# Attention and two gated MLPs on one core: softmax tiles relaid in DRAM, one load a tile, the leftover values loaded once, and a new order of steps

## The chip, the core and the metric

The kernel runs on one core of a Trainium2 chip. The core has a matmul engine (TensorE, "PE" in the profile, its weight loads as "PEld"), three elementwise engines (VectorE "DVE", ScalarE "ACT", GpSimd "POOL") and a queue engine (SyncE "SP") which here issues every transfer between DRAM and the on-chip memory. Sixteen DMA engines carry them out. The metric is device microseconds (us) for one execution. "Slow" and "fast" below mean this time and nothing else.

## What is computed

A batch of 8 sequences of 576 tokens goes through three stages one after the other: attention with 8 heads against keys and values averaged over groups of 8 tokens (so 72 keys a head), an MLP whose hidden layer is gated by a convolution over tokens, and an MLP gated by a learned mix over tokens.

```python
# q, k, v: (8 batches, 8 heads, 576 tokens, 64)
k_p = k.reshape(B, H, 72, 8, D).mean(axis=3); v_p = likewise
attn = softmax(q @ k_p^T / sqrt(D)); attn_out = attn @ v_p
x = attn_out, heads side by side                      # (8, 576, 512)
h = relu(x @ w_in)                                    # 512 -> 1024
x = (h * sigmoid(conv3(h))) @ w_out                   # 1024 -> 512
u, v = halves of gelu(x @ w_in2)                      # 512 -> 512 and 512
v = layernorm(v) * g_ln;  v = w_sg @ v + b_sg         # mix over tokens
out = (u * v) @ w_out2
```

## The kernel before, in words

Work is cut into small steps, each a Python generator that issues a few instructions and yields. A long string, `ORDER`, names which generator goes on next; the first occurrence of a name is its first step, the second its second, and so on. Each engine executes its instructions strictly in that order, the SP queue too, so the string is the schedule of all five queues at once. An instruction that waits holds up all that stand behind it on its own engine.

The names that matter here, for batch b: `s(t,b)` makes the scores of one tile of 128 tokens (the fifth tile, t=4, has 64), the softmax `e` and its normalised copy `en`; its last, ninth, step writes `en` to DRAM. `e(t,b)` brings that tile back with keys on partitions: its first step loads it from DRAM into `xb`, the second turns 32x32 blocks on DVE (L516), the third rounds it on ACT into `eTh` (L520), the fourth makes the rounding error `eTl` on POOL, the fifth does the same for the leftover keys on DVE. Batches 0 and 1 do this with matmuls instead, so all of that holds for batches 2 to 7, 30 tiles. `a(p,b)` multiplies weights and values for a head pair on PE and leaves the MLP's input in `xT`. `q.b` loads a batch's queries in 16 transfers, `p(t,b)` turns them on DVE. `k`, `K` and `v`, `V` load and pool keys and values. With 72 = 64 + 8 keys a head, the last 8 keys of each of the 8 heads form a rest of 64 rows, which `v2.b` loads; it is wanted three times over on different partitions.

`I(f,c)` is the first MLP's input matmul (12 matmuls into `psi`, of which there are two buffers) for 384 tokens with the convolution and gate behind it on ACT and DVE; the DVE instruction of L594 is the last to read the `psi` buffer. `O(f,c)` is its output matmul, nine matmuls. These two fill PE while the attention of a later batch goes on. Letters `y n u d o m` are the second MLP, after all attention.

The DRAM tile `eds[b]` has one row for each token and in it four runs of 192 numbers, one for each quarter of partitions. Its load is four transfers (L510 to L513), one a quarter, each of rows of 192 numbers. The rest of the values is loaded in six transfers (L257 to L260), from four heads each, so that the three copies lie in `raw` at once, 96 partitions by 2; POOL then pools all of it.

Of the kernel before, what the change touches and what calls it, by code (L numbers as in the profile page):

```python
# [8 lines left out]
F32 = mybir.dt.float32  # L9
# [17 lines left out]
def pooled_attention_gated_mlps(  # L27
# [23 lines left out]
    nc = tc.nc  # L51
    w_in, conv_w, w_out, w_in2, w_out2 = (a.bitcast(U32) for a in (w_in, conv_w, w_out, w_in2, w_out2))
    B, H, S, D = q.shape
    POOL = 8
# [4 lines left out]
    NP_ = H // 2  # L59
# [15 lines left out]
    B_DMA = 2  # L75

    const = ctx.enter_context(tc.tile_pool(name="const", bufs=1))
    stat = ctx.enter_context(tc.tile_pool(name="stat", bufs=2))
    work = ctx.enter_context(tc.tile_pool(name="work", bufs=3))
    outp = ctx.enter_context(tc.tile_pool(name="outp", bufs=2))  # L80
    slot = ctx.enter_context(tc.tile_pool(name="slot", bufs=1))
    dram = ctx.enter_context(tc.tile_pool(name="dram", bufs=1, space=bass.MemoryType.DRAM))
    ps1_ctx = ExitStack()
    psum1 = ps1_ctx.enter_context(tc.tile_pool(name="psum1", bufs=1, space=bass.MemoryType.PSUM))

    x2s = [dram.tile([S, DM], F32, name=f"x2s{b}") for b in range(B)]
    eds = [dram.tile([S, 4 * EQ], F32, name=f"eds{b}") for b in range(B)]
    ps2 = {}

    def a_bank():  # L90
        return psum1.tile([128, 512], F32, tag="a", bufs=3, name="psa")

    def i_bank():
        return psum1.tile([128, 512], F32, tag="i", bufs=2, name="psi")

    def o_bank():
        return psum1.tile([128, 512], F32, tag="o", bufs=CT, name="pso")

    def ps_tile():
# [147 lines left out]
    def load_v(b, i, raw):  # L247


        if i < 2:  # L250
            for a in range(4):
                h0, r0 = 4 * i + a % 2, 32 * POOL * (a // 2)
                nc.sync.dma_start(
                    out=raw[32 * a:32 * a + 32, :, :],
                    in_=v[b, h0:h0 + 3:2, r0:r0 + 32 * POOL, :].rearrange("h (j r) d -> j h (r d)", r=POOL))
            return
        for c in range(2):  # L257
            rest = v[b, 4 * c:4 * c + 4, 64 * POOL:S, :].rearrange("h (j r) d -> h j (r d)", r=POOL)
            for x in range(3):
                nc.sync.dma_start(out=raw[32 * x:32 * x + 4 * RJ, c, :], in_=rest)  # L260
# [66 lines left out]
    def t_v(i, b):  # L327
        if b > 1:
            raw = att2.tile([128, 2, 512], F32, tag="raw", name="raw")
        else:  # L330
            raw = staged("q0" if b == 0 and i == 2 else f"st{b}", 2)
        if i == 2 and b < 2:
            nc.sync.dma_start(out=raw[0:64, 0, :],
                              in_=v[b, :, 64 * POOL:S, :].rearrange("h (j r) d -> h j (r d)", r=POOL))
            yield
            ps = a_bank()[0:64, 0:D]
            mm_sum(ps, [(ident[0:64, 0:64], raw[0:64, 0, D * r:D * r + D]) for r in range(POOL)])
            yield
            kv["vr", b] = att1.tile([96, 2, D], F32, tag="vr", name="vr")
            for x in range(3):  # L340
                for c in range(2):
                    nc.scalar.copy(out=kv["vr", b][32 * x:32 * x + 32, c, :], in_=ps[32 * c:32 * c + 32, :])
            return
        load_v(b, i, raw)
        yield
        P = 128 if i < 2 else 96
        ps = None
        if b < 2:
            ps = a_bank()[0:P, 0:2 * D]
            mm_sum(ps, [(ident[0:P, 0:P], raw[0:P, :, D * r:D * r + D]) for r in range(POOL)])  # L350
            yield
        if i < 2 and ("vp", b) not in kv:
            kv["vp", b] = att1.tile([128, NP_, D], F32, tag="vp", name="vp")
        if i == 2:
            kv["vr", b] = att1.tile([96, 2, D], F32, tag="vr", name="vr")
        dst = kv["vr", b] if i == 2 else kv["vp", b][:, 2 * i:2 * i + 2, :]
        if ps is None:
            yield from pool_sum(pool, raw, dst, P)
        else:
            nc.scalar.copy(out=dst, in_=ps.rearrange("p (a d) -> p a d", a=2))  # L360
# [62 lines left out]
    def t_s(t, b):  # L423


        n = TT[t][1]
        qT = qTs.pop((b, t))
        e = sm = m8 = None
        for a in range(2):
            ps = a_bank()  # L430
            for x in range(2):
                p = 2 * a + x
                nc.tensor.matmul(out=ps[0:n, 2 * SP * x:2 * SP * x + 2 * SP], lhsT=qT[:, p, 0:n], rhs=KBT[:, p, :],  # L433
                                 start=True, stop=True)
            yield
            if a == 0:
                e = att2.tile([128, H, SP + 1], F32, tag="e", name="e")
                sm = stat.tile([128, H], F32, tag="sm", name="sm")
                m8 = stat.tile([128, H], F32, tag="mx", name="mx")
                nc.gpsimd.memset(e[:, :, SP:SP + 1], 1e-9)  # L440
                yield
            sv = ps[0:n, 0:4 * SP].rearrange("p (x j) -> p x j", j=SP)
            mx = m8[:, 4 * a:4 * a + 4]
            nc.vector.tensor_reduce(out=mx[0:n], in_=sv, axis=AX.X, op=ALU.max)  # L444
            if b < B_DMA:
                nc.vector.tensor_tensor(out=e[0:n, 4 * a:4 * a + 4, 0:SP], in0=sv, in1=bc(mx[0:n], 2, SP),
                                        op=ALU.subtract)
            else:
                nc.vector.tensor_tensor(
                    out=e[0:n].rearrange("p (x c) j -> p c x j", x=2)[:, 2 * a:2 * a + 2, :, 0:SP],  # L450
                    in0=sv.rearrange("p (c x) j -> p c x j", x=2),
                    in1=bc(mx[0:n].rearrange("p (c x) -> p c x", x=2), 3, SP), op=ALU.subtract)
            yield
        nc.scalar.activation(out=e[0:n, :, 0:SP], in_=e[0:n, :, 0:SP], func=AF.Exp, scale=EXP_SCALE)
        yield
        nc.vector.tensor_reduce(out=sm[0:n], in_=e[0:n], axis=AX.X, op=ALU.add)  # L456
        rs = stat.tile([128, H], F32, tag="rs", name="rs")
        nc.vector.reciprocal(out=rs[0:n], in_=sm[0:n])
        yield
        en = att1.tile([128, H * SP], F32, tag="en", name="en")  # L460
        if b < B_DMA:
            for y in range(2):
                pool.tensor_tensor(
                    out=en[0:n, 0:512].rearrange("p (c y x i) -> p y c x i", c=NP_, y=2, x=2)[:, y],
                    in0=e[0:n].rearrange("p (c x) j -> p c x j", x=2)[:, :, :, 32 * y:32 * y + 32],
                    in1=bc(rs[0:n].rearrange("p (c x) -> p c x", x=2), 3, 32), op=ALU.mult)
            pool.tensor_tensor(out=en[0:n, 512:H * SP].rearrange("p (h j) -> p h j", h=H),
                               in0=e[0:n, :, 64:SP], in1=bc(rs[0:n], 2, RJ), op=ALU.mult)
            es[b, t] = en
            return  # L470
        pool.tensor_tensor(  # L471
            out=en[0:n, 0:512].rearrange("p (y h i) -> p h y i", y=2, h=H),
            in0=e[0:n, :, 0:64].rearrange("p h (y i) -> p h y i", y=2),
            in1=bc(bc(rs[0:n], 2, 2), 3, 32), op=ALU.mult)
        pool.tensor_tensor(
            out=en[0:n, 512:512 + H * RJ].rearrange("p (c x j) -> p x c j", x=2, j=RJ),
            in0=e[0:n, :, 64:SP].rearrange("p (x c) j -> p x c j", x=2),
            in1=bc(rs[0:n].rearrange("p (x c) -> p x c", x=2), 3, RJ), op=ALU.mult)
        yield
        ed = eds[b][TT[t][0]:TT[t][0] + n, :].rearrange("p (a d) -> p a d", a=4)  # L480
        nc.sync.dma_start(out=ed[:, :, 0:128], in_=en[0:n, 0:512].rearrange("p (a d) -> p a d", a=4))
        nc.sync.dma_start(out=ed[:, :, 128:EQ], in_=bc(en[0:n, 512:H * SP], 1, 4))

    def t_e(t, b):
# [26 lines left out]
        for a in range(4):  # L511
            nc.sync.dma_start(
                out=xb[32 * a:32 * a + 32, 0:EQ * G].rearrange("p (g d) -> p g d", d=EQ),  # L513
                in_=eds[b][T, EQ * a:EQ * a + EQ].rearrange("(g i) d -> i g d", i=32))
        yield
        nc.vector.transpose(out=xb[:, 0:EQ * G], in_=xb[:, 0:EQ * G])  # L516
        yield
        m = xb[:, 0:EQ * G].rearrange("p (g c i) -> p c g i", c=NP_ + 2, i=32)
        eh, el = (z[:, :, T].rearrange("p c (g i) -> p c g i", i=32) for z in (eTh, eTl))
        nc.scalar.copy(out=eh, in_=m)  # L520
        yield
# [385 lines left out]
```

## Time and profile before

| | us |
|---|---|
| median of three runs | 1051.41 |
| lowest and highest of them | 1047.47, 1052.53 |
| profiled execution, its own time | 1045.96 |
| its span, first to last instruction | 1044.2 |
| mean granted TensorE clock | 0.974 of full speed |

Busy time in that span: PE 971.6 us (93%), its weight loads 871.4, DVE 673.4 (64%), ACT 440.1 (42%), POOL 363.2 (35%). PE's busy time is an upper picture, since matmuls overlap and their ends are modelled: gaps in it are real, a full slice may still have some slack. The profile's SP rows give the time that issuing a transfer holds the queue; the transfer itself goes on after it. A row's square brackets give the idle time of its engine just before it and what ended that.

### The profile page before, as it was taken

Reading aid. Unit: us, or ns where it says so; the run is one execution under the profiler, and the core shown is the slowest. Engines: PE = TensorE matmul, PEld = TensorE weight load, DVE = VectorE, ACT = ScalarE, POOL = GpSimd, SP = SyncE. Lnnn points to the kernel's source line nnn. Section 1 sums busy time; section 2 is a strip of 40 time slices with the busy share of each in tenths; the row PEclk is TensorE's granted clock in tenths of the full one; section 3 lists DMA queues with packets and bytes.
Section 4 is the critical chain, followed back from the end, with each engine's and each line's share of the span. In section 5 each row is a group of like instructions: output and inputs, shape, how many; then the busy total and the mean of one; then the engine's idle time right before and its main releaser. Section 6 shows DMA issues by size and latency. Waiting matters only on the chain.

```text
span 1044.2 us, 15301 instructions
## 1 busy us (share of the span) xinstructions
PE 971.6 (93%) x5473; PEld 871.4 (83%) x5473; DVE 673.4 (64%) x1190; ACT 440.1 (42%) x872; POOL 363.2 (35%) x485
## 2 busy tenths in 40 slices
PE   5788869999989799899999989999999999999997
PEld 4676758979879699798879869898989898989896
DVE  5868877878778668768559756727272727272523
ACT  3644544756556455556545634313131313130310
POOL 3577587577766466546212201001000100010000
PEclk9899898999999899999999989999999999999999
DMA  9944057366462734514081272232323232312021
GB/s 241 309 132 101 3 129 188 91 151 168 91 169 74 180 87 112 139 39 122 16 234 59 62 199 43 45 92 46 102 45 92 46 102 45 92 23 102 1 81 61
DMA packets 222440, 107.41 MB, mean 103 GB/s; under 512 B 163008, under 2 KB 194780, under 8 KB 222364
## 3 DMA queue, kind: packets, MB, share of 16 engines
q1 hardware_dynamic: 222364, 106.43, 40.4%
q8 instruction: 43, 0.70, 0.3%
q14 instruction: 33, 0.27, 0.1%
HBM read 76.90 MB, written 29.49 MB: 102 GB/s over the span
## 4 chain that ended last, share of the span: by engine, by line
PE 65%; DVE 12%; DMA 7%; POOL 6%; SPq 4%; issue 3%; ACT 3%; DVEq 0%; POOLq 0%; ACTq 0%
PE ps L122 21%; PE psi L116 10%; PE ps L110 6%; PE ps L109 6%; PE ps L111 6%; PE psa L116 3%; PE pso L109 3%; PE pso L111 3%; PE pso L110 3%; DMA xb<-eds 3%; PE psa L433 1%; DVE psi L587 1%; DVE eTh L153 1%; DVE sm L456 1%; DVE psi L588 1%
## 5 line engine op out<-in xcount | busy, mean ns | idle before, releaser
L153 POOL TENSOR_TENSOR hg<-g,hg 128x384 fp32r<-128x384 f32 x96 | 99.4, 1037 | 120.5 <-ACT hg L597 110.2
L767 POOL TENSOR_SCALAR rstd<-mv 128x2 f32<-128x2 f32 (+1 forms) x20 | 8.1, 407 | 367.1 <-DVE mv L764 367.1
L122 PE MATMUL ps<-w2sh,v 128*128 128x288 f32 x512 | 94.3, 296 | 0.0
L587 DVE SCALAR_TENSOR_TENSOR psi<-h,coef,psi 128x384 f32<-128x384 f32 x96 | 58.8, 613 | 47.6 <-ACT psi L585 47.2
L813 DVE SCALAR_TENSOR_TENSOR y<-ps,coef,bsg 128x576 f32<-128x576 f32 x32 | 26.2, 818 | 89.7 <-PE ps L122 89.7
L818 ACT CAST gt<-y 128x576 fp32r<-128x576 f32 (+2 forms) x48 | 23.0, 512 | 128.2 <-DVE y L815 128.2
L122 PEld LDWEIGHTS ps<-w2sh,v 128*128 128x128 f32 x512 | 77.1, 189 | 0.0
L575 ACT ACTIVATE h<-psi 128x386 f32<-128x386 f32 (+1 forms) x96 | 47.2, 491 | 67.3 <-PE psi L116 66.7
L590 ACT ACTIVATE psi<-psi 128x384 f32<-128x384 f32 x96 | 45.5, 474 | 63.1 <-DVE psi L588 62.7
L597 ACT CAST hg<-g 128x384 fp32r<-128x384 f32 x96 | 48.6, 508 | 44.5 <-DVE g L594 37.0
L588 DVE SCALAR_TENSOR_TENSOR psi<-h,coef,psi 128x384 f32<-128x384 f32 x96 | 59.8, 623 | 3.4
L433 PE MATMUL psa<-KBT,qT 128*128 128x144 f32 (+1 forms) x320 | 55.0, 301 | 5.1 <-DVE qT L418 1.6
L594 DVE SCALAR_TENSOR_TENSOR g<-psi,h 128x384 f32<-128x384 f32 x96 | 51.9, 542 | 11.0 <-ACT psi L590 10.6
L585 ACT ACTIVATE psi<-h,coef 128x384 f32<-128x384 f32 x96 | 56.3, 586 | 3.1
L433 PEld LDWEIGHTS psa<-KBT,qT 128*128 128x128 f32 (+1 forms) x320 | 46.0, 185 | 12.7 <-issue 5.1
L122 PE MATMUL ps<-w2sl,v 128*128 128x288 f32 x256 | 54.8, 296 | 0.0
L799 ACT ACTIVATE u<-ps 128x576 f32<-128x576 f32 x32 | 19.9, 652 | 75.6 <-PE ps L122 75.6
L276 POOL TENSOR_TENSOR raw<-raw 128x512 f32<-128x512 f32 (+2 forms) x36 | 44.0, 1224 | 17.7 <-DMA raw<-in_v_dram 8.2
L516 DVE STREAM_TRANSPOSE xb<-xb 128x768 f32<-128x768 f32 (+1 forms) x30 | 26.8, 895 | 35.9 <-DMA xb<-eds 35.6
L444 DVE TENSOR_REDUCE mx<-psa 128x4 f32<-128x288 f32 (+1 forms) x80 | 35.1, 439 | 17.3 <-PE psa L433 17.1
L471 POOL TENSOR_TENSOR en<-e,rs 128x512 f32<-128x512 f32 (+1 forms) x30 | 31.9, 1063 | 41.3 <-DMA eds<-en 22.5
L153 POOL TENSOR_TENSOR eTl<-xb,eTh 128x512 fp32r<-128x512 f32 (+1 forms) x30 | 36.3, 1211 | 23.8 <-ACT eTh L520 18.0
(409 smaller groups left out, 3016.4 us busy)
## 6 DMA issues: line engine op xcount, KB each, us to landing
xb<-eds SPq DMA_DIRECT2D x96, 96.0 KB
xb<-x2s SPq DMA_DIRECT2D x128, 72.0 KB
x2s<-ob SPq DMA_DIRECT2D x32, 256.0 KB
res<-x2s SPq DMA_DIRECT2D x16, 512.0 KB
out_dram<-ob SPq DMA_DIRECT2D x16, 512.0 KB
qb<-in_q_dram SPq DMA_DIRECT2D x96, 72.0 KB
raw<-in_k_dram SPq DMA_DIRECT2D x12, 512.0 KB
raw<-in_v_dram SPq DMA_DIRECT2D x48, 128.0 KB
```

Source lines behind the costliest of these rows:

```text
L109: nc.tensor.matmul(out=out_, lhsT=ah, rhs=bh, start=first, stop=False)
L110: nc.tensor.matmul(out=out_, lhsT=al, rhs=bh, start=False, stop=False)
L111: nc.tensor.matmul(out=out_, lhsT=ah, rhs=bl, start=False, stop=last)
L116: nc.tensor.matmul(out=out_, lhsT=a, rhs=b_, start=(i == 0), stop=(i == n - 1))
L122: nc.tensor.matmul(out=ps[:, hf, 0:HS], lhsT=a, rhs=b_[:, hf * HS:(hf + 1) * HS], start=(i == 0), stop=(i == n - 1),)
L153: eng.tensor_tensor(out=out, in0=in0, in1=hi.bitcast(F32), op=ALU.subtract)
L433: nc.tensor.matmul(out=ps[0:n, 2 * SP * x:2 * SP * x + 2 * SP], lhsT=qT[:, p, 0:n], rhs=KBT[:, p, :], start=True, stop=True)
L585: nc.scalar.activation(out=y, in_=tap(1), func=AF.Copy, scale=cw(1, f))
L587: nc.vector.scalar_tensor_tensor(out=y, in0=tap(0), scalar=cw(0, f), in1=y, op0=ALU.mult, op1=ALU.add)
L588: nc.vector.scalar_tensor_tensor(out=y, in0=tap(2), scalar=cw(2, f), in1=y, op0=ALU.mult, op1=ALU.add)
L594: nc.vector.scalar_tensor_tensor(out=go, in0=y, scalar=1.0, in1=tap(1), op0=ALU.add, op1=ALU.mult)
L597: nc.scalar.copy(out=hg[:, 0, f, :], in_=g)
```

## The change

Three things change in the code. The softmax tiles get one DRAM tile for each batch and token tile, with four blocks, one for each quarter of partitions, and in a block one row of 192 numbers a token. The load is now one transfer: partition i of a quarter takes G consecutive rows of its block (G=4, or 2 for the 64-token tile), so that the 32x32 blocks that DVE turns hold every fourth token. The reading order behind the turn follows: ACT, POOL and DVE read `xb` with the token group innermost, at a distance of 192 numbers (768 bytes), and write `eTh` and `eTl` in token order. The writes to DRAM keep their number and the length of their runs. The rest of the values is loaded once, in one transfer of 64 rows, pooled on 64 partitions into a new tile `vq`, and six ACT copies of 32x64 spread it (batches 0 and 1 did it in that way already, with matmuls for the pooling). And `ORDER` is another string: the same steps but for one more of each `v2.b`, with b from 2 to 7, in another sequence from the 129th step on.

```diff
-ORDER = '''...
- (around e1.5) I6.5 v0.6 s2.5 I5.5 v1.6 v2.6 p4.5 s2.5 I5.5 s3.5 s3.5 I6.5 s2.5 O7.4 I5.5 I6.5 s2.5 e1.5 O7.4 s3.5 I7.5 I6.5 I5.5 k0.7 I6.5 s2.5 I6.5 s3.5 q.6 I6.5 I7.5 e1.5 I0.6 V.5
+ORDER = '''...
+ (around v2.6) I2.5 p3.5 I3.5 s1.5 v1.6 v0.6 I3.5 s2.5 s1.5 I4.5 v2.6 O6.4 O6.4 I3.5 I4.5 s1.5 s2.5 v1.6
...
+ (around e1.5) I4.5 e1.5 I5.5 O7.4 q.6 I6.5 s2.5 I5.5 I5.5 s2.5 s3.5 I5.5 s3.5 I6.5 I5.5 I7.5 s3.5 V.5 I6.5 s3.5 s4.5 s4.5 V.5 e1.5 I7.5
...
-    eds = [dram.tile([S, 4 * EQ], F32, name=f"eds{b}") for b in range(B)]
+    eds = {(b, t): dram.tile([4 * n, EQ], F32, name=f"eds{b}{t}")
+           for b in range(B_DMA, B) for t, (_, n) in enumerate(TT)}
...
     def load_v(b, i, raw):
-        if i < 2:
-            for a in range(4):
...
-            return
-        for c in range(2):
-            rest = v[b, 4 * c:4 * c + 4, 64 * POOL:S, :].rearrange("h (j r) d -> h j (r d)", r=POOL)
-            for x in range(3):
-                nc.sync.dma_start(out=raw[32 * x:32 * x + 4 * RJ, c, :], in_=rest)
...
+        if i == 2:
+            nc.sync.dma_start(out=raw[0:64, 0, :],
+                              in_=v[b, :, 64 * POOL:S, :].rearrange("h (j r) d -> h j (r d)", r=POOL))
+            yield
+            vq = att1.tile([64, D], F32, tag="vq", name="vq")
+            yield from pool_sum(pool, raw[:, 0:1], vq.rearrange("p (a d) -> p a d", a=1), 64)
+            yield
+            kv["vr", b] = att1.tile([96, 2, D], F32, tag="vr", name="vr")
+            for x in range(3):
+                for c in range(2):
+                    nc.scalar.copy(out=kv["vr", b][32 * x:32 * x + 32, c, :], in_=vq[32 * c:32 * c + 32, :])
+            return
...
-        ed = eds[b][TT[t][0]:TT[t][0] + n, :].rearrange("p (a d) -> p a d", a=4)
+        ed = eds[b, t].rearrange("(a p) d -> p a d", a=4)
...
-        for a in range(4):
-            nc.sync.dma_start(
-                out=xb[32 * a:32 * a + 32, 0:EQ * G].rearrange("p (g d) -> p g d", d=EQ),
-                in_=eds[b][T, EQ * a:EQ * a + EQ].rearrange("(g i) d -> i g d", i=32))
+        nc.sync.dma_start(out=xb[:, 0:EQ * G], in_=eds[b, t].rearrange("(p g) d -> p (g d)", g=G))
...
-        m = xb[:, 0:EQ * G].rearrange("p (g c i) -> p c g i", c=NP_ + 2, i=32)
-        eh, el = (z[:, :, T].rearrange("p c (g i) -> p c g i", i=32) for z in (eTh, eTl))
+        m = xb[:, 0:EQ * G].rearrange("p (g c i) -> p c i g", c=NP_ + 2, i=32)
+        eh, el = (z[:, :, T].rearrange("p c (i g) -> p c i g", i=32) for z in (eTh, eTl))
```

Counted over the 30 tiles, `I` and `O` first steps (each some 2 us of PE) that the string puts between a tile's load and its turn: 49 before, 72 after (one for 13 tiles before; two is the least after). Between a tile's write and its load: 77 before, 108 after. Between `q.b` and `p0.b`, batches 2 to 7: 3, 3, 4, 5, 4, 4 before and 4, 5, 6, 6, 4, 6 after. Before, `v2.3`, `v2.4`, `v2.5` and `v2.6` load one `I` or `O` step ahead of the loads of `e0.2`, `e1.3`, `e1.4` and `e1.5`, and no other transfer is issued between the two; after, `v2.3`, `v2.4` and `v2.5` come behind `e1.2`, `e1.3` and `e1.4`, and `v2.6` three steps ahead of `e1.5`. After, the 16 transfers of `q.3`, `q.4`, `q.5` and `q.7` stand four such steps ahead of the loads of `e1.2`, `e1.3`, `e1.4` and `e1.6`.

## Rows read from the trace of the kernel before

**Rows 1.** The page's 40 slices of the span, PE and granted clock, in tenths.
```profile
PE   5788869999989799899999989999999999999997
PEclk9899898999999899999999989999999999999999
```

**Rows 2.** Busy time by stretch: length, then PE, PEld, DVE, ACT, POOL, clock, DMA share, GB/s.
```profile
0.00:128.00 128.00, 98.08 (x588) 82.47 (x588) 97.52 (x176) 62.98 (x148) 75.94 (x113) 0.92 0.62 160
128.00:506.00 378.00, 347.28 (x1825) 310.74 (x1825) 284.94 (x538) 214.20 (x432) 243.14 (x313) 0.97 0.50 121
506.00:624.00 118.00, 111.34 (x543) 97.33 (x543) 81.51 (x139) 59.20 (x121) 21.31 (x21) 0.97 0.43 122
624.00:1044.20 420.20, 414.94 (x2522) 380.91 (x2520) 209.43 (x338) 103.77 (x172) 22.80 (x40) 1.00 0.26 63
```

**Rows 3.** Timeline of PE, 128 to 506 us: start, length, work, [idle before, releaser].
```profile
158.45 0.69 PE L116 MATMUL psi<-xh,wi5hl 128*128 128x388 f32 x1 [6.52 <-DVE g L594]
...
228.93 0.54 PE L116 MATMUL psi<-xh,wi3hl 128*128 128x386 f32 x1 [2.03 <-DVE g L594]
...
285.06 0.44 PE L116 MATMUL psi<-xh,wi5hl 128*128 128x388 f32 x1 [1.85 <-DVE g L594]
...
353.57 0.69 PE L116 MATMUL psi<-xh,wi1hl 128*128 128x386 f32 x1 [7.58 <-DVE g L594]
...
428.64 0.44 PE L116 MATMUL psi<-xh,wi6hl 128*128 128x388 f32 x1 [2.20 <-DVE g L594]
```

**Rows 4.** Who waited for whom, one line (total, times, longest), and DVE's timeline.
```profile
DVE xb L516 <- DMA xb<-eds: 35.6, 19, 6.3
...
152.16 0.98 DVE L516 STREAM_TRANSPOSE xb<-xb 128x768 f32<-128x768 f32 x1 [5.01 <-DMA xb<-eds]
...
348.58 0.98 DVE L516 STREAM_TRANSPOSE xb<-xb 128x768 f32<-128x768 f32 x1 [6.26 <-DMA xb<-eds]
...
423.45 0.71 DVE L418 STREAM_TRANSPOSE qT<-qb 128x512 f32<-128x512 f32 x1 [3.56 <-DMA xb<-eds]
```

**Rows 5.** Timeline of the SP queue: start, time the issues hold it, transfer, count.
```profile
337.82 4.04 SPq L260 DMA_DIRECT2D raw<-in_v_dram  x6
341.99 1.79 SPq L512 DMA_DIRECT2D xb<-eds  x4
...
409.91 11.36 SPq L391 DMA_DIRECT2D qb<-in_q_dram  x16
```

**Rows 6.** Three short stretches behind gaps, columns as in rows 2.
```profile
158.40:164.00 5.60, 5.55 (x17) 5.55 (x18) 3.39 (x7) 2.26 (x5) 2.40 (x4) 0.50 0.63 129
228.90:234.00 5.10, 5.07 (x18) 4.86 (x19) 4.48 (x9) 2.76 (x6) 2.31 (x3) 0.67 0.85 212
353.60:360.00 6.40, 6.40 (x22) 5.56 (x23) 3.31 (x8) 2.06 (x5) 4.37 (x6) 0.59 0.86 159
```

**Rows 7.** The chain that ended last, in order of time: start, length, piece.
```profile
189.32 2.12 PE psi L116 x12
...
343.35 5.11 DMA xb<-eds
...
501.29 1.81 DMA xb<-eds
```

**Rows 8.** Instructions by line: count, ns min/median/max, first and last start, shapes.
```profile
L512 SPq DMA_DIRECT2D xb<-eds x120: 302/430/1862, 146.1 to 501.3; - x120
...
L276 POOL TENSOR_TENSOR raw<-raw x36: 719/1286/1733, 66.3 to 418.2; 128x512 f32<-128x512 f32 x24, 64x256 f32<-64x256 f32 x6, 96x512 f32<-96x512 f32 x6
...
L342 ACT COPY vr<-psa x12: 185/202/206, 29.7 to 49.3; 32x64 f32<-32x64 f32 x12
...
L153 POOL TENSOR_TENSOR eTl<-xb,eTh x30: 733/1290/1516, 154.5 to 504.9; 128x512 fp32r<-128x512 f32 x24, 128x256 fp32r<-128x256 f32 x6
```

**Rows 9.** Two DVE sums by line, columns as in rows 8: strided input, contiguous input.
```profile
L274 DVE TENSOR_REDUCE kp<-st x2: 1011/1442/1872, 4.4 to 7.0; 128x128 f32<-128x1024 f32 x1, 64x64 f32<-64x512 f32 x1
...
L456 DVE TENSOR_REDUCE sm<-e x40: 709/754/764, 16.6 to 493.1; 128x8 f32<-128x584 f32 x32, 64x8 f32<-64x584 f32 x8
```

More of the change, by code (lines that the diff above doesn't have):

```diff
@@ L247, in load_v @@
     def load_v(b, i, raw):
-        if i < 2:
-            for a in range(4):
-                h0, r0 = 4 * i + a % 2, 32 * POOL * (a // 2)
-                nc.sync.dma_start(
-                    out=raw[32 * a:32 * a + 32, :, :],
-                    in_=v[b, h0:h0 + 3:2, r0:r0 + 32 * POOL, :].rearrange("h (j r) d -> j h (r d)", r=POOL))
-            return
-        for c in range(2):
-            rest = v[b, 4 * c:4 * c + 4, 64 * POOL:S, :].rearrange("h (j r) d -> h j (r d)", r=POOL)
-            for x in range(3):
-                nc.sync.dma_start(out=raw[32 * x:32 * x + 4 * RJ, c, :], in_=rest)
+        for a in range(4):
+            h0, r0 = 4 * i + a % 2, 32 * POOL * (a // 2)
+            nc.sync.dma_start(
+                out=raw[32 * a:32 * a + 32, :, :],
+                in_=v[b, h0:h0 + 3:2, r0:r0 + 32 * POOL, :].rearrange("h (j r) d -> j h (r d)", r=POOL))
     def staged(name, n, where=None):
@@ L343, in t_v @@
             return
+        if i == 2:
[10 more added lines that the diff above has]
+            return
         load_v(b, i, raw)
         yield
-        P = 128 if i < 2 else 96
+        P = 128
         ps = None
@@ L353, in t_v @@
             kv["vp", b] = att1.tile([128, NP_, D], F32, tag="vp", name="vp")
-        if i == 2:
-            kv["vr", b] = att1.tile([96, 2, D], F32, tag="vr", name="vr")
-        dst = kv["vr", b] if i == 2 else kv["vp", b][:, 2 * i:2 * i + 2, :]
+        dst = kv["vp", b][:, 2 * i:2 * i + 2, :]
         if ps is None:
@@ L510, in t_e @@
         xb = att1.tile([128, 4 * EQ], F32, tag="xb", name="xb")
-        for a in range(4):
-            nc.sync.dma_start(
-                out=xb[32 * a:32 * a + 32, 0:EQ * G].rearrange("p (g d) -> p g d", d=EQ),
-                in_=eds[b][T, EQ * a:EQ * a + EQ].rearrange("(g i) d -> i g d", i=32))
+        nc.sync.dma_start(out=xb[:, 0:EQ * G], in_=eds[b, t].rearrange("(p g) d -> p (g d)", g=G))
         yield
```

2 lines of the change are left out of this document (1 added, 1 removed).

## Prediction, before the result was known

> **What bounds the kernel now.** I read the page's slices first, then busy time by stretch, then PE's timeline, then the engines and the queue that stand behind its gaps. The slices [rows 1] show PE full from the 24th slice on: the second MLP. By stretch [rows 2] PE is busy 414.9 of 420.2 us there, so the new sequence of its steps has nothing to take. Up to 624 us PE stands still for 29.9, 30.7 and 6.7 us in the three stretches. The change's loads belong to batches 2 to 7, that is to the stretch from 128 to 506 us, where DVE (75%), POOL (64%), ACT (57%) and the DMA engines (50%) all have room on average. What counts is the 30.7 us of gaps and what the clock does behind them.
>
> The five longest of these gaps after 150 us [rows 3] sum to 20.2 us, and each ends when DVE's L594 gives a `psi` buffer back. L594 is late because DVE, which goes strictly in order, stands at something else. Before the first and the fourth gap it stands for 5.01 and 6.26 us at the turn of a softmax tile whose load hasn't landed; such waits sum to 35.6 us over 19 tiles [rows 4]. Why the load is late is on the queue [rows 5]: the six transfers of the values' rest hold SP for 4.04 us, then the tile's own four for 1.79 us, and only then is its data under way. The load itself took 5.11 us in that place and 1.81 us at 501 us, where nothing was ahead of it [rows 7]. The first four gaps of rows 3 all fall on loads that the string of before puts right behind such a rest: `e0.2`, `e1.3`, `e1.4`, `e1.5`. The fifth has another cause: DVE waits 3.56 us at L418 [rows 4]. The row names the tile load, but L418 reads `qb`, and `q.7`'s 16 transfers hold SP from 409.91 for 11.36 us [rows 5], so I put it down to the query load.
>
> The clock adds to it. [...] PE works there all the time, so 5.60 x 0.50 + 5.10 x 0.33 + 6.40 x 0.41 = 7.1 us are lost.
>
> **The change, part by part.** *Fewer issues.* Three of four loads a tile go: 30 x 3 x 0.43 us = 39 us of SP time [rows 8]. What one load of the whole tile holds SP for, no row shows; I take 0.43 us from the same line, with 0.30 and 1.86 us, that line's shortest and longest, as bounds; at either bound the four together took as long or longer. The rest costs one issue instead of six: at 4.04 / 6 = 0.67 us each, 6 x 5 x 0.67 = 20 us. So some 59 us of 378 on SP are gone, none of it PE time in itself. It counts only where an issue stands ahead of a late load: 1.3 us of the load's own and 3.4 us of the rest's, 4.7 us in each of the four places.
>
> *Fewer rows to move.* A row of four times the length and a third of the rest's bytes (64 rows for 192). I book nothing more for it: its effect is in the gap.
>
> *The new order.* An `I` step is 2.12 us of PE [rows 7]; an `O` step I take as the same. Between load and turn the string now has 72 such steps for 30 tiles where it had 49: 5.1 us instead of 3.5 us on average, and never under 4.2 us, where 13 tiles had 2.1 us. Between write and load it is 7.6 instead of 5.4 us. A load of 1.8 to 5.1 us [rows 7] now fits, where 2.1 us couldn't hold it. At the four places the rest is either behind the tile's load or, for `e1.5`, three steps (6.4 us) ahead. So I count those gaps as gone: 6.52 + 2.03 + 1.85 + 7.58 = 18.0 us [rows 3], and the half clock behind them, 7.1 us. `q.7` gets six steps instead of four up to its turn, 4.2 us more against a gap of 2.20 us and a wait of 3.56 us: gone as well. Sum of the gains: 18.0 + 7.1 + 2.2 = 27.3 us.
>
> *What comes next in line.* `q.3`, `q.4`, `q.5` and `q.7` are now four steps, 8.5 us, ahead of the loads of `e1.2`, `e1.3`, `e1.4` and `e1.6`. Their 16 issues can hold SP for 11.36 us [rows 5], so those loads can be 2.9 us late at the queue. With two to three steps (4.2 to 6.4 us) up to the turn and a load of 1.8 to 5.1 us, DVE is late by between nothing and 2.9 + 5.1 - 4.2 = 3.8 us. Writes of `en` stand behind `q` too, and POOL's next `en` behind them. I take 1 us a place, near the low end since the queue is freed of 59 us elsewhere: 4 us back, bounds 0 and 15.
>
> *Strided reads.* ACT, POOL and DVE now read `xb` at a distance of 768 bytes from number to number. No row has that on ACT or POOL. The nearest is DVE's sum of L274, with a distance of 256 bytes: 1872 / 1024 = 1.83 ns a number against 754 / 584 = 1.29 of L456, which reads in sequence [rows 9]. The difference of 0.54 ns gives 0.41 us on ACT (768 numbers), 0.28 us on POOL (512) and 0.14 us on DVE (256), 0.83 us a tile. It counts where `a` waits for the last tile of a half, twelve places: 0 to 10 us. I take 2 us, since none of the long gaps of PE ends on `eTh` or `eTl` [rows 3].
>
> [...]
>
> *The rest on POOL and ACT.* Half the numbers a partition: L276 goes from 1.29 towards its shortest, 0.72 us [rows 8], and two shorter sums with it; about 1 us a batch, off the path. ACT gets 6 x 0.20 us [rows 8] a batch, 7.3 us in all, under an ACT that is 57% busy; with no cover that would be 7.3 us. It also gets a wait that wasn't there: the copies wait for POOL's sums, and behind them on ACT stand the Relu and tanh of the running `I` steps, which DVE and then `psi` and PE wait for. The wait is between none and one POOL sum of 1.29 us, six times: 0 to 7.7 us. I take 1 us, since POOL has room.
>
> *Elsewhere.* The string differs from its 129th step on, within the first 128 us too, and in the passage to the second MLP. I can't read a sign from it and book 0, with one gap of the largest size seen, 7.6 us, to either side.
>
> Sum: 27.3 - 4 - 2 - 1 = 20.3 us. Against the profiled execution's own 1045.96 us that is 1025.7 us. The median of the runs shown is 5.4 us above it; from 1051.4 the forecast is 1031 us.
>
> **Rivals.** *The query loads hold the tiles mildly:* the worst lateness of 3.8 us at all four places, with a half clock of 1.7 us behind each [rows 6], costs 4 x 5.5 - 4 = 18 us more: 1049 us. For it: the 11.36 us. Against: before, `q.3` was already one step ahead of `e1.2` and no long gap of rows 3 is there. *They take the rest's place in full (the slower side):* where a load lands more than two steps after its turn in the string, DVE stops, then L594, then PE. At the price of the fourth gap, 7.58 + 2.6 us, four places cost 40.8 us instead of 4: 1068 us. It decides from the point where `q` holds SP for well over 8.5 us and its data are still ahead of the tile's. *Strided reads on the path of every tile:* 24 x 0.83 + 6 x 0.42 = 22 us instead of 2: 1051 us. [...] *The order opens one new long gap* of 10.2 us with its clock, early or at the passage: 1041 us. *It does more:* all of the 30.7 us of the stretch and the clock go, 37.8 us: 1014 us.
>
> **How the numbers follow.** Forecast, with its near surroundings from 1018 to 1044 us: 0.57. More than that: 0.10. One new gap: 0.06. Query loads mildly: 0.11. Strided reads on the path: 0.09. Query loads in full: 0.07. The range from 1013 to 1050 us leaves out the slower side, the upper half of the two cases around 1050 and a little at the low end. A change under 0.5%, 5 us, can't be told from none in a measurement of this kernel. Faster by more: 0.57 + 0.10 + 0.06 and a quarter of the 0.20 around 1050, 0.78; the same: 0.14; slower: 0.08.
>
> **What would show it.** Right: no PE gap over 2 us on L594 at the turns of `e0.2`, `e1.3`, `e1.4`, `e1.5`; DVE's wait on the tile loads down from 35.6 us to under 10; clock at full from 128 to 506 us but for short dips; PE's idle time there around 12 us. Wrong: DVE waiting at the turns of `e1.2`, `e1.3`, `e1.4`, `e1.6` right after 16 query issues; `eTl` much longer than 1.29 us, or L520 longer than it was, with PE waiting on them; ACT idle before the rest's copies; or the gain gone in the first 128 us.

## The result, and the profile after

The changed kernel takes 1010.43 us (median of four runs, 1010.28 to 1013.18), the kernel before in the same series 1049.44 us: a ratio of 0.9634, interval 0.9597 to 0.9671. That is 39.0 us, where the prediction had 20.3. Between the two profiled executions, 1045.96 and 1010.28 us, it is 35.7 us.

The page's slices of PE and the granted clock, in tenths, in the kernel after:

```profile
PE   5798899999998999999899899999999999999997
PEclk9899999999999999999999999999999999999999
```

Against [rows 1], only the first of the 8s in the clock row is left, and PE is full from the second quarter on, but for an 8 here and there. Busy time by stretch, after (length, then PE, PEld, DVE, ACT, POOL, clock, DMA share, GB/s):

```profile
0.00:128.00 128.00, 101.25 (x634) 86.47 (x635) 105.53 (x203) 71.55 (x168) 88.65 (x133) 0.96 0.68 174
128.00:506.00 378.00, 367.35 (x1944) 330.75 (x1943) 281.79 (x540) 246.83 (x481) 245.60 (x299) 0.99 0.51 128
506.00:624.00 118.00, 112.41 (x621) 101.72 (x620) 88.25 (x150) 57.63 (x109) 17.94 (x20) 0.97 0.32 82
624.00:1008.50 384.50, 379.31 (x2280) 346.76 (x2278) 186.09 (x301) 90.93 (x151) 19.16 (x34) 1.00 0.26 66
```

PE's busy time multiplied by the granted clock says how much full-clock work PE got done in a stretch. Before [rows 2] that is 98.08 x 0.92 = 90.2, 347.28 x 0.97 = 336.9 and 111.34 x 0.97 = 108.0 us; after it is 97.2, 363.7 and 109.0 us. The kernel after is thus ahead by 7.0 us at the end of the first stretch, by 26.8 more at the end of the second and by 1.0 more in the third: 34.8 of the 35.7 us (the clock's two digits leave up to 1.0 us open in the first difference and 3.6 in the second). Nearly everything was won before the second MLP: from its first product, at 616.98 us before and 581.54 us after, to the end it takes 427.2 and 427.0 us.

The gaps of PE over 1 us between 120 and 506 us, after (start, length, work, [idle before, releaser]):

```profile
125.15 0.80 PE L112 MATMUL pso<-w6hl,hg 128*128 128x512 f32 x1 [3.44 <-POOL w6hl L154]
...
141.43 0.45 PE L117 MATMUL psi<-xh,wi5hl 128*128 128x388 f32 x1 [1.13 <-DVE g L596]
...
268.99 0.44 PE L117 MATMUL psi<-xh,wi6hl 128*128 128x388 f32 x1 [1.37 <-DVE g L596]
...
320.94 0.45 PE L117 MATMUL psi<-xh,wi0hl 128*128 128x386 f32 x1 [3.69 <-DVE g L596]
...
488.11 0.45 PE L117 MATMUL psi<-xh,wi0hl 128*128 128x388 f32 x1 [2.97 <-DVE g L596]
```

None of the five gaps of [rows 3] is left. Two new ones of 3.69 and 2.97 us are there; DVE's only two waits on tile loads over 1 us come later than the first of them, at 331.47 and 343.12 us, and long before the second. Who waited for whom, after (total, times, longest):

```profile
PE psi L117 <- DVE g L596: 10.1, 6, 3.7
...
DVE xb L518 <- DMA xb<-eds: 2.6, 2, 1.3
```

DVE's waits on tile loads fell from 35.6 us [rows 4] to 2.6.

### The profile page after: what moved, and what is told of

Its sections match the earlier page's. It is cut to its first block, busy times and chain, and to the rows that moved or that the text cites. A ratio compares the mean times of both kernels' runs of the same rounds, so it can differ in the third digit from the quotient of the medians.

```text
span 1008.5 us, 15021 instructions
## 1 busy us (share of the span) xinstructions
PE 960.3 (95%) x5473; PEld 865.7 (86%) x5473; DVE 661.7 (66%) x1190; ACT 466.9 (46%) x908; POOL 371.3 (37%) x485
## 4 chain that ended last, share of the span: by engine, by line
PE 76%; DVE 3%; POOL 2%; issue 2%; ACT 1%; DMA 1%; SPq 0%; POOLq 0%; DVEq 0%; ACTq 0%
PE ps L123 22%; PE psi L117 14%; PE ps L110 6%; PE ps L111 6%; PE ps L112 6%; PE pso L110 5%; PE pso L112 5%; PE pso L111 5%; PE psa L117 3%; PE psa L438 2%; DMA eds<-en 1%; POOL eTl L154 1%; POOL hg L154 1%; DVE psi L589 1%; ACT eTh L522 0%
## 5 line engine op out<-in xcount | busy, mean ns | idle before, releaser
L154 POOL TENSOR_TENSOR hg<-g,hg 128x384 fp32r<-128x384 f32 x96 | 98.2, 1025 | 123.0 <-ACT hg L599 120.4
L154 POOL TENSOR_TENSOR eTl<-xb,eTh 128x512 fp32r<-128x512 f32 (+1 forms) x30 | 50.4, 1679 | 40.4 <-ACT eTh L522 39.1
L596 DVE SCALAR_TENSOR_TENSOR g<-psi,h 128x384 f32<-128x384 f32 x96 | 52.0, 544 | 10.3 <-ACT psi L592 6.9
L765 DVE BATCH_NORM_STATS2 st<-vg 128x6 f32<-128x512 f32 x36 | 24.4, 678 | 36.9 <-ACT vg L760 36.9
L449 DVE TENSOR_REDUCE mx<-psa 128x4 f32<-128x288 f32 (+1 forms) x80 | 35.6, 446 | 16.7 <-PE psa L438 16.1
L522 ACT CAST eTh<-xb 128x768 fp32r<-128x768 f32 (+1 forms) x30 | 41.8, 1393 | 4.2 <-DVE xb L518 4.2
L271 POOL TENSOR_TENSOR raw<-raw 128x512 f32<-128x512 f32 (+1 forms) x36 | 40.3, 1120 | 3.5 <-DMA raw<-in_k_dram 1.7
```

The lines of the kernel that those rows point to most:

```text
L154: eng.tensor_tensor(out=out, in0=in0, in1=hi.bitcast(F32), op=ALU.subtract)
L596: nc.vector.scalar_tensor_tensor(out=go, in0=y, scalar=1.0, in1=tap(1), op0=ALU.add, op1=ALU.mult)
```

## The experiments

The runs were made on several chips. Each ratio, and each gain against the kernel before, is taken from runs of the kernel before on the same chip (their medians lie from 1046.8 to 1050.6 us).

**Which part does it: the order or the code?** The first kernel is the one before with the changed string of steps alone.

```diff
-ORDER = '''(the steps as before)'''
+ORDER = '''(the steps as after)'''
```

> The kernel before with the new string of steps only; tiles in DRAM, four loads a tile and six loads of the rest as before (the fifth step of each v2 does nothing). Theory A, the new order makes the gain because a load now has two to four I or O steps up to its turn: some 1018 us, 30 of the 39 us gained, waits of DVE on tile loads under 10 us. Theory B, the fewer issues make the gain and the order only fits them: at least 1035 us, since the queue has its 59 us of issues back, and waits of DVE on tile loads over 20 us.

Measured: 1022.60 us, 0.9736 [0.9708, 0.9764]. The second has all the changed code under the old string (with one step more for `v2.b`, which needs it).

```diff
-ORDER = '''(the steps as after)'''
+ORDER = '''(the steps as before, one more v2.b behind the fourth)'''
```

> The changed code under the string of before (the fifth step of each v2 put right behind its fourth). Theory A (order): the gaps at the turns of e0.2, e1.3, e1.4, e1.5 get shorter by at most the 4.7 us of issues ahead of the load and the first 128 us stay as they were: 1035 us or more. Theory B (fewer issues): the four long gaps go, 1025 us or less.

Measured: 1026.87 us, 0.9782 [0.9756, 0.9807]. The order alone brings 27.7 us and the code alone 23.5, both together 39. They cure partly the same thing. Both times lie between the two expectations, the first nearer to theory A and the second 2 us above theory B's. DVE's waits on tile loads, order alone and code alone; with the order alone they stay above the 10 us that theory A had:

```profile
DVE xb L516 <- DMA xb<-eds: 15.1, 6, 6.1
```

```profile
DVE xb L518 <- DMA xb<-eds: 8.1, 11, 1.4
```

**Which part of the code?** The kernel before with the rest loaded and pooled once, old tiles and old order:

```diff
-        for c in range(2):
-            rest = v[b, 4 * c:4 * c + 4, 64 * POOL:S, :].rearrange("h (j r) d -> h j (r d)", r=POOL)
-            for x in range(3):
-                nc.sync.dma_start(out=raw[32 * x:32 * x + 4 * RJ, c, :], in_=rest)
+            nc.sync.dma_start(out=raw[0:64, 0, :],
+                              in_=v[b, :, 64 * POOL:S, :].rearrange("h (j r) d -> h j (r d)", r=POOL))
... (the pooling on 64 partitions and ACT's copies, as in the change)
```

> The kernel before with the values' rest loaded once, pooled once and copied by ACT; tile layout, four loads a tile and the old order of steps stay. Theory R (under the old order what makes the tile loads late is the six transfers of the rest that stand ahead of them): nearly all of what the changed code under the old order gained (1026.9 against 1050.3 us) comes back, 1026 to 1032 us, and DVE's waits on tile loads fall from 35.6 to 10 to 15 us. Rival T (the four issues of each tile load are the cause): the gain is small, 1042 to 1050 us, and DVE's waits stay above 25 us.

Measured: 1027.29 us, 0.9778 [0.9744, 0.9811]. The other half, the kernel before with the tiles' new layout and one load a tile:

```diff
-        for a in range(4):
-            nc.sync.dma_start(
-                out=xb[32 * a:32 * a + 32, 0:EQ * G].rearrange("p (g d) -> p g d", d=EQ),
-                in_=eds[b][T, EQ * a:EQ * a + EQ].rearrange("(g i) d -> i g d", i=32))
+        nc.sync.dma_start(out=xb[:, 0:EQ * G], in_=eds[b, t].rearrange("(p g) d -> p (g d)", g=G))
... (the tiles in DRAM and the reading order behind the turn, as in the change)
```

> The kernel before with the softmax tiles in DRAM in the new layout and one load a tile; the rest in six transfers and the old order stay. Theory R: 1042 to 1049 us, DVE's waits on tile loads above 25 us, with the long ones still behind the rest. Rival T: 1026 to 1032 us and waits under 15 us. A third case, each of the two edits enough by itself: both kernels at 1026 to 1034 us.

Measured: 1052.26 us, 1.0013 [1.0000, 1.0027], which is above theory R's range. Under the old order the rest is the whole of the code's gain, and the one load a tile brings no time. DVE's waits on tile loads do fall, from 35.6 to 21.9 us, where theory R had over 25; whether the dearer strided reads take back what that gives, no run under the old order shows. Its queue and its longest gap, in the place of [rows 5], show what is left: the six transfers of the rest still stand ahead of the load, which now has one issue instead of four and still comes too late.

```profile
340.41 4.01 SPq L261 DMA_DIRECT2D raw<-in_v_dram  x6
344.54 0.38 SPq L512 DMA_DIRECT2D xb<-eds  x1
```

```profile
357.20 0.69 PE L117 MATMUL psi<-xh,wi1hl 128*128 128x386 f32 x1 [8.92 <-DVE g L592]
```

**And under the new order?** The changed kernel with the old tiles and their four loads, the rest loaded once:

```diff
-        nc.sync.dma_start(out=xb[:, 0:EQ * G], in_=eds[b, t].rearrange("(p g) d -> p (g d)", g=G))
+        for a in range(4):
+            nc.sync.dma_start(
+                out=xb[32 * a:32 * a + 32, 0:EQ * G].rearrange("p (g d) -> p g d", d=EQ),
+                in_=eds[b][T, EQ * a:EQ * a + EQ].rearrange("(g i) d -> i g d", i=32))
... (the tiles in DRAM and the reading order behind the turn, as before)
```

> The changed kernel with the softmax tiles as before: one DRAM tile a batch, four loads a tile, reads of xb in sequence; new string and the rest of the values in one transfer. Theory A, the new sequence leaves the loads enough room and one load a tile is worth little: 1010 to 1014 us. Rival, the 39 us of issues on SP and the short rows count: 1020 us or more.

Measured: 1011.40 us, 0.9654 [0.9627, 0.9681], 1 us from the changed kernel (whose ratio is 0.9634, with overlapping intervals). And the changed kernel with the rest in six transfers and the new tiles:

```diff
-            nc.sync.dma_start(out=raw[0:64, 0, :],
-                              in_=v[b, :, 64 * POOL:S, :].rearrange("h (j r) d -> h j (r d)", r=POOL))
...
+            for x in range(3):
+                nc.sync.dma_start(out=raw[32 * x:32 * x + 4 * RJ, c, :], in_=rest)
... (the pooling on 96 partitions by 2, without ACT's copies, as before)
```

> The changed kernel with the rest of the values loaded in six transfers of 96 rows by 2 and pooled on POOL as before, no ACT copies; new string, one load a tile. Theory A (order): the six issues now stand behind the tile loads, so little is lost: 1010 to 1015 us. Theory B (issues): 3.4 us of the queue at each of six places come back with gaps and clock, 1025 us or more.

Measured: 1021.47 us, 0.9728 [0.9697, 0.9759]. Theory A, that the rest costs little once the order keeps it away from the tile loads, has fallen: it is worth 11 us here too, though theory B's 1025 us is not reached. DVE's waits on tile loads grow from 2.6 to 6.3 us, and the gap of 3.69 us is one of 5.09 here; the rest of the 11 us lies in shorter gaps and clock dips (from 128 to 506 us PE is busy for 362.29 us at a clock of 0.98, against 367.35 at 0.99), which this run doesn't put down to one step.

```profile
328.86 0.69 PE L117 MATMUL psi<-xh,wi0hl 128*128 128x386 f32 x1 [5.09 <-DVE g L592]
```

```profile
DVE xb L514 <- DMA xb<-eds: 6.3, 4, 2.9
```

So four pairs of kernels that differ in the tiles alone stand within 2 us (1050.6 and 1052.3, 1027.3 and 1026.9, 1022.6 and 1021.5, 1011.4 and 1010.4; as ratios within 0.2%), and the rest alone makes 23 us under the old order and 11 under the new.

**What of the six transfers costs: the time on SP or the data?** Two kernels split it, both made from the one with the rest alone. In the first the single copy comes in six transfers:

```diff
-            nc.sync.dma_start(out=raw[0:64, 0, :],
-                              in_=v[b, :, 64 * POOL:S, :].rearrange("h (j r) d -> h j (r d)", r=POOL))
+            for h0, h1 in ((0, 2), (2, 3), (3, 4), (4, 6), (6, 7), (7, 8)):
+                nc.sync.dma_start(out=raw[RJ * h0:RJ * h1, 0, :],
+                                  in_=v[b, h0:h1, 64 * POOL:S, :].rearrange("h (j r) d -> h j (r d)", r=POOL))
```

> As the kernel with the rest alone, but the single copy of the rest comes in six transfers of one or two heads each, so that SP issues six times as before and only a third of the bytes are moved. If the time that SP is held by the issues makes the tile loads late: 1040 to 1048 us, and DVE waits of 4 to 6 us right behind the rest. If the bytes and rows that are moved ahead of the tile's do it: 1026 to 1033 us, within 3 us of the kernel with the rest alone.

Measured: 1036.59 us, 0.9870 [0.9846, 0.9894]. In the second all the bytes come in three transfers:

```diff
-            nc.sync.dma_start(out=raw[0:64, 0, :],
-                              in_=v[b, :, 64 * POOL:S, :].rearrange("h (j r) d -> h j (r d)", r=POOL))
+            for dst in (raw[64:128, 0, :], raw[0:64, 1, :], raw[0:64, 0, :]):
+                nc.sync.dma_start(out=dst,
+                                  in_=v[b, :, 64 * POOL:S, :].rearrange("h (j r) d -> h j (r d)", r=POOL))
```

> As the kernel with the rest alone, but the same 64 rows are fetched three times (two of the copies go to places that nothing reads), each in one transfer: as many bytes and rows as before in three issues, about 2.0 us of SP instead of 0.66 (one), 3.0 (six small ones) and 4.04 us (before). If the time on SP sets the price, it goes with these numbers: one transfer gave 1027.3 and six small ones 1036.6 us, 9.3 us for 2.3 us more of SP a batch, so about 1032.5 us here (1030 to 1036). If the bytes and rows that are moved ahead of the tile's set it, they are as before: 1041 to 1049 us.

Measured: 1036.20 us, 0.9851 [0.9797, 0.9905]. Both land between the two theories. The queue, and DVE at the tile's turn behind the same rest; first the rest alone, then six small transfers, then three of the whole:

```profile
322.94 0.66 SPq L339 DMA_DIRECT2D raw<-in_v_dram  x1
324.67 1.74 SPq L516 DMA_DIRECT2D xb<-eds  x4
...
328.46 0.98 DVE L520 STREAM_TRANSPOSE xb<-xb 128x768 f32<-128x768 f32 x1 [0.84 <-DMA xb<-eds]
```

```profile
333.61 3.00 SPq L340 DMA_DIRECT2D raw<-in_v_dram  x6
336.73 1.75 SPq L517 DMA_DIRECT2D xb<-eds  x4
...
340.48 0.98 DVE L521 STREAM_TRANSPOSE xb<-xb 128x768 f32<-128x768 f32 x1 [1.95 <-DMA xb<-eds]
```

```profile
330.72 1.97 SPq L340 DMA_DIRECT2D raw<-in_v_dram  x3
332.93 1.73 SPq L517 DMA_DIRECT2D xb<-eds  x4
...
339.16 0.98 DVE L521 STREAM_TRANSPOSE xb<-xb 128x768 f32<-128x768 f32 x1 [3.90 <-DMA xb<-eds]
```

SP alone can't be it: three large transfers hold SP for 1 us less than six small ones, and DVE waits 1.95 us longer for the tile behind them. From the tile's own first issue to its turn it is 3.79, 3.75 and 6.23 us, and 6.59 us before [rows 4, 5]; over the four places it is 3.75 to 4.56 us with six small transfers, 5.30 to 6.23 with three and 5.94 to 6.63 before. So the tile itself lands some 1.6 to 2.0 us later, on average, behind the threefold data. The data alone can't be it either: six small transfers bring the same 64 rows as one, and the kernel is 9.3 us slower. In this place the wait goes 0.84, 1.95, 3.90 and, before [rows 4], 6.26 us: both count, the data for more of it here. The signs that were expected did not come, though. With six small transfers the waits right behind the rest are 0.5 to 1.95 us, not 4 to 6; the two longest, 4.49 and 4.28 us at 235.25 and 364.53 us, are at loads further back on the queue, and why these are late the run doesn't show. So how the 9.3 us arise, and how the 23 us divide, is not settled, since the kernel before also pools three times the rows on POOL and has none of ACT's copies.

**Do the strided reads cost anything?** The changed kernel, with ACT, POOL and DVE reading `xb` in sequence; the tokens of a tile then stand in another order than the tile in DRAM has them.

```diff
-        m = xb[:, 0:EQ * G].rearrange("p (g c i) -> p c i g", c=NP_ + 2, i=32)
-        eh, el = (z[:, :, T].rearrange("p c (i g) -> p c i g", i=32) for z in (eTh, eTl))
+        m = xb[:, 0:EQ * G].rearrange("p (g c i) -> p c g i", c=NP_ + 2, i=32)
+        eh, el = (z[:, :, T].rearrange("p c (g i) -> p c g i", i=32) for z in (eTh, eTl))
```

> The changed kernel with ACT, POOL and DVE reading xb in sequence again, as before; the tokens of a tile then stand in another order in eTh and eTl, so the attention output is not the one wanted. Theory A, the slower reads (eTh 1.59 instead of 0.83 us, eTl 1.94 instead of 1.29 us) lie beside PE's work: 1007 to 1010 us. Rival, they are on the path of the twelve places where a waits for a half: 12 x 1.4 = 17 us less, some 994 us.

Measured: 1010.17 us, 0.9627 [0.9595, 0.9660]: the same as the changed kernel. The instructions by line (count, ns min/median/max, first and last start, shapes), first the changed kernel, then this one:

```profile
L522 ACT CAST eTh<-xb x30: 586/1590/1637, 134.1 to 476.1; 128x768 fp32r<-128x768 f32 x24, 128x384 fp32r<-128x384 f32 x6
L154 DVE TENSOR_TENSOR eTh<-xb,eTh x30: 587/616/1795, 135.8 to 476.7; 32x256 fp32r<-32x256 f32 x24, 32x128 fp32r<-32x128 f32 x6
L154 POOL TENSOR_TENSOR eTl<-xb,eTh x30: 794/1938/1976, 135.8 to 477.1; 128x512 fp32r<-128x512 f32 x24, 128x256 fp32r<-128x256 f32 x6
```

```profile
L522 ACT CAST eTh<-xb x30: 497/822/840, 135.8 to 476.4; 128x768 fp32r<-128x768 f32 x24, 128x384 fp32r<-128x384 f32 x6
L154 POOL TENSOR_TENSOR eTl<-xb,eTh x30: 734/1287/1557, 136.7 to 477.5; 128x512 fp32r<-128x512 f32 x24, 128x256 fp32r<-128x256 f32 x6
L154 DVE TENSOR_TENSOR eTh<-xb,eTh x30: 417/1056/2517, 137.2 to 477.0; 32x256 fp32r<-32x256 f32 x24, 32x128 fp32r<-32x128 f32 x6
```

The reads are dear, 0.77 us a tile on ACT and 0.65 on POOL, and all of it lies beside other work.

**What came from the start?** The kernel before, with the new sequence for its first 467 steps (up to `I0.1`) and the old one behind.

```diff
-ORDER = '''(the steps as before)'''
+ORDER = '''(the first 467 steps as after, the others in the sequence of before)'''
```

> The kernel before with only the first 467 steps of its string in the new sequence (up to the first step of I0.1, at 110 to 122 us); what is left follows in the sequence of before. Theory A, the new sequence makes the start shorter by itself and the gain stays: 9 us less than before, some 1041 us, with I0.1 starting near 113 us. Rival, the start only brings work forward that the later steps then wait for: 1047 us or more, with I0.1 early and I0.2 at 170 us or later.

Measured: 1039.66 us, 0.9926 [0.9903, 0.9949]: 7.1 us from a part of the string in which no softmax tile is loaded from DRAM. Most of it comes from two places. The first is 104 to 118 us, columns as above; before, then with the new start:

```profile
104.00:118.00 14.00, 10.67 (x42) 9.30 (x43) 11.56 (x23) 7.58 (x18) 4.26 (x5) 0.63 0.00 1
```

```profile
104.00:118.00 14.00, 12.75 (x72) 10.87 (x73) 13.37 (x24) 7.93 (x20) 9.30 (x14) 1.00 0.16 48
```

Before, PE was busy for 10.67 us of 14 at a mean granted clock of 0.63: 10.67 x 0.63 = 6.7 us of work. With the new start it is 12.75 us at a clock of 1.00: 6.0 us more, of which 2.1 are idle time and 3.9 the clock. The half clock follows a gap here too. PE stands still for 2.47 us up to 108.43 us, and from there to 116.10 us it is busy for 7.21 of 7.67 us at a granted clock of 0.50:

```profile
108.43 0.58 PE L502 MATMUL psa<-ident,en 128*32 128x128 f32 x2 [2.47 <-DVE eTl L153]
...
108.43:116.10 7.67, 7.21 (x27) 6.58 (x28) 7.02 (x13) 2.80 (x7) 4.26 (x5) 0.50 0.00 0
```

The second place is a gap of 4.10 us, the longest of PE in the first 128 us but for the wait before its first matmul, with half clock behind it (0.50 from 76 to 78 us). The gap, then the stretch around it before and with the new start:

```profile
74.58 0.50 PE L111 MATMUL pso<-w0hl,hg 128*128 128x512 f32 x1 [4.10 <-POOL e L440]
...
72.00:80.00 8.00, 5.42 (x20) 4.90 (x21) 3.70 (x6) 0.47 (x1) 6.09 (x9) 0.79 0.55 131
...
72.00:80.00 8.00, 8.00 (x47) 6.68 (x47) 7.69 (x16) 5.33 (x12) 6.71 (x10) 1.00 0.29 63
```

There it is 5.42 x 0.79 = 4.3 us of work against 8.0. Smaller gaps between and behind the two places take back some 2.5 us of these 9.7. The part of the string behind it, unchanged, keeps its waits on tile loads (31.5 us).

One single step was tried as the cause at the start: `t0`, whose last step on POOL makes the `w0hl` that PE's instruction at 74.58 us reads (the row names a memset that POOL ended beside it), moved ahead of the pooling sums of the third batch.

```diff
-K.1 V.1 k0.2 K.1 ... k2.2 k2.2 t0 I1.0
+K.1 V.1 t0 k0.2 K.1 ... k2.2 k2.2 I1.0
```

> The kernel before with one step moved: the last step of t0 (POOL's rounding error of the first output weights) goes ahead of POOL's sums for k0.2, k1.2 and k2.2. Theory A, PE's gap of 4.10 us at 74.6 us is POOL standing at these sums, and with it the 3.4 us of half clock go: 4 to 6 us less, some 1045 us. Rival, the keys of batch 2 are late in turn or PE waits for the next thing: within 2 us of before.

Measured: 1049.48 us, 1.0024 [1.0004, 1.0045]. The gap went, and a longer one opened behind it: POOL's sums come later, it then stands 2.62 us at a load of values (1.68 before) and comes to `en` at 83.51 instead of 80.50 us:

```profile
84.76 1.11 PE L493 MATMUL psa<-ident,en 128*128 128x128 f32 x4 [7.46 <-POOL en L463]
```

**A further version.** In the changed kernel the steps around its four remaining long gaps were moved: the weights' steps `t6` and `V.2`, some steps of `I6.5` and `I6.9`, and at the passage `g4` ahead of `l0` and `l1`.

```diff
-s2.2 s0.2 V.2 t6 s1.2 ... v0.3 I1.1 t6 O6.0 ... e0.2 s1.2 I0.1
+s2.2 s0.2 t6 s1.2 ... t6 v0.3 I1.1 O6.0 ... e0.2 s1.2 V.2 I0.1
-s4.5 V.5 e1.5 I7.5 V.5 ... e1.5 I7.5 I6.5 e1.5 e1.5 I7.5 I6.5 v2.6
+s4.5 V.5 I6.5 e1.5 I6.5 I7.5 V.5 ... e1.5 I7.5 e1.5 e1.5 I7.5 v2.6
-a3.7 a3.7 I7.9 y0.0 I6.9 I7.9 I6.9 I7.9 w4
+a3.7 a3.7 I6.9 I7.9 y0.0 I6.9 I7.9 I7.9 w4
-l1 g4 l0 g4 l1 l0 g4 g4 ...
+l1 g4 g4 g4 g4 ... l0 l1 l0 l1
```

> The changed kernel with a few steps moved at its four remaining gaps of 3.4, 3.7, 3.0 and 4.1 us (at 125, 321, 488 and 582 us): t6's last step ahead of a sum of v0.3, POOL's part of V.2 behind it, tanh and gate of I6.5 and I6.9 ahead of what stood before them on ACT and DVE, and g4's last steps ahead of the weights of l0 and l1. Theory A, each gap is an engine standing at something that is not urgent, and some 2 us of each and the half clock behind go: 999 to 1003 us. Rival, something else is late right behind: 1008 us or more.

Measured: 1005.47 us, 0.9612 [0.9589, 0.9635], between the two expectations. It is 5 us under the changed kernel's median, but that was measured on another chip, and as ratios (0.9612 and 0.9634) the intervals overlap; against the kernel with the old tiles, which ran on the same chip, it is 5.9 us. The two gaps on L596 shrink to 1 us, that at the passage (4.07 us at 581.54) to 2.08, the first moves to the next weight, and smaller ones appear:

```profile
134.10 0.50 PE L112 MATMUL pso<-w7hl,hg 128*128 128x512 f32 x1 [2.50 <-POOL w7hl L154]
...
320.29 0.44 PE L117 MATMUL psi<-xh,wi0hl 128*128 128x386 f32 x1 [1.07 <-DVE g L596]
...
486.59 0.45 PE L117 MATMUL psi<-xh,wi0hl 128*128 128x388 f32 x1 [1.02 <-DVE g L596]
```

## Why the prediction was wrong

The direction was right, the size was half of what came, and 1010 us lies under the range. One step failed and two terms were mis-sized. In full-clock work the changes against the profiled execution before are these:

| Term | predicted, us | in the traces, us |
|---|---|---|
| 128 to 506 us, gaps and clock | 27.3 | 26.8, costs included |
| costs of query loads, strides, copies | -7 | none seen |
| first 128 us and passage ("Elsewhere") | 0 | 7.0 + 1.0 |
| added to the forecast time, runs over their profile | +5.4 | about 0 |

Of the 20.7 us between the forecast of 1031.1 and the median of 1010.43 us, 8.0 are in "Elsewhere", 6.5 in the costs (26.8 us won where 27.3 - 7 = 20.3 were forecast) and 5.3 in the base; 0.9 us are left over. The rival "It does more" is nearest in number (1014 us), but not the cause: it had all gaps of the second stretch gone, and 10.7 us of them are left.

**The gains.** The five gaps and the half clock behind them were read rightly: idle time of PE from 128 to 506 us goes from 30.7 to 10.7 us, 20.1 us less where the five gaps make 20.2, and the clock's loss from 347.28 x 0.03 = 10.4 to 367.35 x 0.01 = 3.7 us, where 7.1 was booked from the three stretches of [rows 6]. The agreement is partly luck: two new gaps of 3.69 and 2.97 us opened, and shorter ones that I had left as they were went. The forecast of some 12 us of idle time and of waits under 10 us came true.

**"Elsewhere: 0" is the step that failed.** I wrote that I couldn't read a sign from the string's changed start. The sign was in the rows: the granted clock of the first stretch was 0.92 [rows 2], the lowest of the four, which alone is 98.08 x 0.08 = 7.8 us lost, PE stood still there for 29.9 us, and the string differs in that stretch. I had listed the long gaps only after 150 us; the gaps of 4.10 and 2.47 us at 74.58 and 108.43 us, each with half clock behind it, stand ahead of that. After, the clock costs 101.25 x 0.04 = 4.1 us there and the idle time is 26.8 us, so that the 7.0 us are 3.8 of clock and 3.2 of gaps. The run with the new start alone shows that this part is worth 7.1 us.

**The costs that did not come.** *The query loads* (4 us booked, two rivals): they do hold SP, for 8.44 to 9.55 us in the four places, and the tile loads behind them are issued late, but the tiles are in time. SP and DVE in the first place, after:

```profile
131.30 8.55 SPq L396 DMA_DIRECT2D qb<-in_q_dram  x16
139.96 0.43 SPq L516 DMA_DIRECT2D xb<-eds  x1
...
146.90 0.94 DVE L518 STREAM_TRANSPOSE xb<-xb 128x768 f32<-128x768 f32 x1
```

The load is issued at 139.96 and the tile turned at 146.90 us with no wait before it; so are those issued at 200.55, 256.00 and 385.09 us, turned at 205.92, 262.02 and 390.55 us. Both rivals on the query loads are dead. Only behind `q.6`, which the prediction didn't name, DVE waits 1.29 us for a tile, at 331.47 us. *The strided reads* (2 us booked, one rival): I put 0.41 us a tile on ACT and 0.28 on POOL, and it is 0.77 and 0.65 us. On POOL the 1.29 us of `eTl` [rows 8] become 1.94, so my estimate from DVE's row did not hold. Yet the price in time is 0.3 us, within the interval. The price was too low and the cover complete. *ACT's copies* (1 us booked): 36 copies of 0.24 us, and ACT waited for POOL's sum once, for 1.0 us:

```profile
L349 ACT COPY vr<-vq x36: 227/243/249, 90.9 to 390.5; 32x64 f32<-32x64 f32 x36
```

**The base.** The profiled execution before was 5.4 us under the median of three runs; I added these 5.4 us to the forecast. The runs of after stand at 1010.28 to 1013.18 us with the profiled one at 1010.28, so they don't stand over their profile. The scatter of before (1046.59 to 1052.53) doesn't carry over.

**The place of the gain.** I booked all of it to the new order and nothing to the smaller rest beyond the gaps. The runs show two cures for one illness: the rest alone gives 23.3 us, the order alone 27.7, both 39. In the stretch for which I booked 27.3 us to the order, the order alone wins less. Order alone, then code alone:

```profile
128.00:506.00 378.00, 360.83 (x1892) 324.03 (x1893) 293.04 (x538) 220.31 (x446) 238.94 (x302) 0.97 0.49 125
...
128.00:506.00 378.00, 360.44 (x1917) 323.88 (x1916) 289.92 (x556) 247.96 (x484) 252.88 (x313) 0.99 0.50 122
```

In full-clock work that is 350.0 - 336.9 = 13.1 us for the order and 356.8 - 336.9 = 19.9 us for the code, against 26.8 for both (the clock's digits leave up to 3.6 us open in each). With the order alone DVE still waits 15.1 us for tiles, up to 6.1 at a time. So that the gaps are gone "by the new order" was half of it: the smaller rest does as much or more, and my sum came out only because the change has both. And the 39 us of SP time from one load a tile, which I said count in four places, bring nothing that is clear of noise: with the rest ahead of it unchanged, a single issue leaves the time where it was (1052.3 us), and with the rest made smaller four issues come early enough (1011.4 us).

## What to carry to other kernels

Multiply busy time by the granted clock, stretch by stretch, before looking at single gaps: a stretch with a clock well under 1 has its loss even where its gaps look short (2.47 us of gap here had 3.6 us of clock lost behind it), and an edit of the order that reaches into it can give it back. Where a transfer comes late, ask what stands ahead of it on the queue, how long that holds the queue and how much data it brings, before making the late transfer itself cheaper. A dearer instruction on an engine that has its work in time cost nothing here, and a forecast should set such a cost from its cover, not from its price.

## What the runs showed of the hardware

Reading 128x768 numbers at a distance of 768 bytes takes ACT 1.59 us instead of 0.82, nearly twice; POOL pays half as much again for 128x512 (1.94 for 1.29 us). DVE's shortest subtraction of the leftover keys goes from 0.42 to 0.59 us (both are of 32x256), but the median over all falls from 1.06 to 0.62; why, the runs don't tell. The same 16 query transfers hold SP for between 8.44 and 9.65 us after, and 8.92 and 13.30 us before.
